# Attention, then two expert layers on one core: filler matmuls, decay products, state zeros and the order at attention's end are placed otherwise

## The chip, the cores and the metric

The kernel runs on one core of a Trainium2 chip. Five engines work side by side, each through its own list of instructions in the order in which they were written: PE (TensorE, matmuls and transposes), DVE (VectorE), ACT (ScalarE), POOL (GpSimd) and SP (SyncE, which here only issues DMAs). The metric is device microseconds of one execution, lower is better. Rows of the profile count microseconds from the first instruction.

## The reference

Three layers in a row. Only their core is shown.

```python
# attention: B=2, H=8 heads, S=768 positions, D=48
for t in range(S):
    state = alpha[:, :, t, :, None] * state + einsum('bhd,bhe->bhde', k[:, :, t], v[:, :, t])
    y[:, :, t] = einsum('bhd,bhde->bhe', q[:, :, t], state)
x = y in rows of 384                       # 1536 tokens
# first expert layer: 8 experts, top 1, 384 -> 1024 -> 384
e = argmax(x @ w_gate); gate = softmax(x @ w_gate)[e]
x = gate * (relu(x @ w1[e]) @ w2[e])       # up to `capacity` tokens per expert
# second expert layer: noisy top 2 of 8
logits = x @ w_gate + log1p(exp(x @ w_noise)) * noise
out = sum over the 2 best experts of softmax weight * (relu(x @ w1[e]) @ w2[e])
```

## The kernel before

**Attention in chunks.** The positions of a batch are cut into 6 chunks of 128, so there are 12 chunks, numbered i = 0 to 11 (batch 0 first). Within a chunk the recurrence is turned into matrix products: `decays` makes running products of alpha with scans on DVE (one forward and one backward over each half chunk) and multiplies them into k and q. For one piece of the sequence (one, two or three chunks; the first has one chunk, then one, two, two, three and three) it issues, on DVE: a first scan and the product with k's first half (`times(V, k6, kn, w6, 0)`), a second scan and the product with q's second half, two small instructions, two more scans, and then the products of k's second half and q's first half with the last two scans. In the very first piece the product with q's second half comes late, so that three products stand in a row. A copy of the piece's chunk-start decays (`V.tensor_copy(z2v[:, :, 0], as_[:, m:])`) comes before the first scan, in the pieces for which ACT has not made it (`filled`).

**What a chunk does on PE.** `scores(i)` transposes the products of k (4 transposes) and multiplies k and q products (8 matmuls, each in the trace as two halves, so 16 rows); ACT copies both out, and GpSimd sets the upper triangle to zero (`affine_select`). `state(i)` updates the carried state, which ACT or DVE writes into `att`, a tile whose state part is set to zero at the start. `mix(i)` makes the chunk's output, copied out by ACT as `yT` (the line `A.activation(yT..., y[:HR, :], AF.Copy)`). `r1_logits(j)` multiplies `yT` of chunk j with an identity and the gate's weights; ACT copies the tokens out, and a DVE reduction (`gates`) makes the gate logits. `route1` then finds each token's expert and its row in eight steps (maximum, index and one-hot on DVE; an exponential on ACT; ranks on PE; sums on DVE; and the scatter of the rows to DRAM by indirect DMAs from GpSimd).

**The order.** Nothing is scheduled by a program: `PATTERNS[i]` is a string per chunk, and each letter issues one thing: S scores of the next chunk, D a step of the decays, T the state, L the logits of chunk i - 1, R a step of the routing, W a quarter of a split of the first expert's weights (ACT copies the high part, GpSimd or DVE makes the low part by subtraction), M the mix. `FXR` is such a string for the end of attention: x a step of `first_x` (which gathers the first expert's tokens on PE: three steps for the early chunks' rows, then one per late chunk 8 to 11), R a routing step, l the logits of chunk 11. Because every engine works its list in order, a letter's place decides what stands behind it on all engines.

**The fillers.** `warm(n)` issues n matmuls of 512 columns on a tile of zeros; nothing reads them. `WARM0` of them stand at the start, `WARM2` = 10 behind the first scores, `FILL` behind chunk 0's mix, `WARM1` = 2 at the end of attention.

**The expert layers.** Behind attention each layer works expert by expert: the hidden product, then the second product, both with weights split into a high and a low part (three matmuls for one). The change leaves these layers alone.

Of the kernel before, what the change touches and what calls it, by code (L numbers as in the profile page):

```python
# [12 lines left out]
ALU = mybir.AluOpType  # L13
# [5 lines left out]
HR = 112  # L19
# [11 lines left out]
P1 = C1 // T1  # L31
R = N
SPARE = E * R
WARM0 = 34
NF, ND = F // 128, DM // 128
IW = HR + E
PIECES = [(0, 0, 2), (0, 2, 2), (0, 4, 2), (1, 0, 3), (1, 3, 3)]
# [2 lines left out]
MASKS = "G" * 12  # L40
STATES = "AAAAAAAAVVVV"
DECAYS = "444444440000"
FILL = (20,)
S0 = 1
WARM1 = 2
WARM2 = 10
FXR = "xRRxRRlxRRRRRxxRxRR"
EARLY = 8
WE = "GGGGVVVVVVVVVGGG"
PATTERNS = (  # L50
    "SDDTDDM", "SDDTLDDM", "SDDTLDDM", "SDDTLRRRDDM", "SDDTLDDM", "SRRDTLRRRDDDM",
    "SDDTLRRRDDM", "WSDDTWLDDMW", "WSRRWTRRRWLRRRWMW", "RWSRWTRRRWLWMW", "STLRRRWWMW", "RRRRRLRRRM")
LATE = (0, 4)
LZ = 0
LR = (5, 6, 7, 5, 7, 8)
# [12 lines left out]
def body(tc, ap, cap, dbg=False, stop=False):  # L68
    nc = tc.nc
    V, A, G, PE = nc.vector, nc.scalar, nc.gpsimd, nc.tensor  # L70
    with ExitStack() as ctx:
# [46 lines left out]
        qkv, vts = {}, {}  # L118

        piece_of, room = {}, {}  # L120
        a_at, at_ = {}, 0
# [4 lines left out]
        def load_piece(b, c0, n):  # L126
            parts_ = PARTS[PIECES.index((b, c0, n))]
            w = n * 512
            a6, k6, q6 = s6([128, w + sum(1 + 8 * m for _, _, m in parts_)]), s6([128, w]), s6([128, w])
            oa = o = 0  # L130
            for (b, c, m) in parts_:
                wa, v = 520 * m + 1, m * 512
                mine = (a6[:, oa:oa + wa], *(x[:, o:o + v].rearrange("r (h j) -> r h j", h=2) for x in (k6, q6)))
                nc.sync.dma_start(mine[0], ap["as"][:, a_at[b, c]:a_at[b, c] + wa])
                at = 128 * 512 * (b * NC + c)
                for x, name in zip(mine[1:], ("ks", "qs")):
                    nc.sync.dma_start(x.rearrange("r h j -> r (h j)"),
                                      ap[name][at:at + 128 * v].rearrange("(r w) -> r w", w=v))
                qkv[b, c] = [x[:HR] for x in mine]
                room[b, c] = ((b, c0), o, w)  # L140
                for i in range(c, c + m):
                    piece_of[b, i] = (b, c)
                oa, o = oa + wa, o + v
# [8 lines left out]
        NCK = B * NC  # L152
# [20 lines left out]
        att = s6([128, 4 * IW + 128 + 8 * HR])  # L173
# [15 lines left out]
        z5 = const([HR, 12, 64], "z5")  # L189
        A.activation(z5, zs["z3"], AF.Copy)  # L190
        z2s = (zs["z2"], z5)
        V.memset(att[:HR, 4 * IW + 128:], 0.0)
        warm(WARM0)
        load_v(*PIECES[0])
        for a in PIECES[1:3]:
# [28 lines left out]
        begun, filled = [], []  # L224

        def decays(b, c0, n):
# [12 lines left out]
            w1v = w6[:, 0].rearrange("r (s j) -> r s j", j=64)  # L239
            w2v = w6[:, 1].rearrange("r (s j) -> r s j", j=64)  # L240

            def times(eng, src, dst, x, h):
                o = dst.rearrange("r (s h j) -> r s h j", h=2, j=64)[:, :, h, :]
                eng.tensor_tensor(o, src[:, h].rearrange("r (s j) -> r s j", j=64),
                                  x[:, h].rearrange("r (s j) -> r s j", j=64), op=ALU.mult)

            first, k_ = not begun, len(begun)
            z2v = z2s[k_ % 2][:, :m, :]
            z2 = z2v.rearrange("r s j -> r (s j)")
            if (b, c0) not in filled:  # L250
                V.tensor_copy(z2v[:, :, 0], as_[:, m:])
            begun.append((b, c0))
            V.tensor_tensor_scan(w6[:, 0, ::-1], a6[:, 1:w + 1][:, ::-1], z1[:, ::-1], 0.0, op0=ALU.mult, op1=ALU.add)
            times(V, k6, kn, w6, 0)
            yield
            V.tensor_tensor_scan(w6[:, 1], a6[:, w:2 * w], z2, 0.0, op0=ALU.mult, op1=ALU.add)
            if not first:
# [12 lines left out]
                                 op0=ALU.mult, op1=ALU.add)  # L270
            if first:
                times(V, q6, qn, w6, 1)
            times(V, k6, kn, v6, 1)
            yield
            times(V, q6, qn, v6, 0)
            if todo and todo[0][:2] in qkv:
                b2, c2, n2 = todo[0]
                filled.append((b2, c2))
# [100 lines left out]
        def r1_logits(j, first=True):  # L379
            js, row, l, k = grp[j]  # L380
            yT = yTs.pop(j)
            lg = pm()
            lv = lg[:, :4 * IW].rearrange("p (g n) -> p g n", g=4)
            for gp in range(4):
                PE.matmul(lv[:, gp, :], yT[:, gp, :], idw[:, gp, :], start=True, stop=True)  # L385
            def gates():
                V.tensor_reduce(l[:, k, :], lv[:, :, HR:].rearrange("p g n -> p n g"), axis=AX.X, op=ALU.add)


            if j == NCK - 1:  # L390
                gates()
            by = lambda x: x.rearrange("p (g a e) -> p g a e", g=4, a=2)
            for ab in range(2):
                A.activation(by(row[:, k, :DM])[:, :, ab, :], lv[:, :, ab * 64:ab * 64 + 48], AF.Copy)
            if j < NCK - 1:
                gates()
            if j >= EARLY and first:
                t = late[j] = sb([128, 2 * DM + C1], "b6", 5, F32R)
                A.activation(t[:, :DM], row[:, k, :DM], AF.Copy)
                G.tensor_tensor(t[:, DM:2 * DM], row[:, k, :DM], t[:, :DM].bitcast(F32), op=ALU.subtract)  # L400
            if dbg:
                nc.sync.dma_start(ap["xdbg"][j * 128:(j + 1) * 128], row[:, k, :DM])
# [653 lines left out]

        si_, slots = hb([128, C1], I32), hb([128, C1])
        G.iota(si_, pattern=[[1, C1]], base=0, channel_multiplier=0)
        A.activation(slots, si_, AF.Copy)
        for i in range(S0):  # L1060
            need(i)
# [483 lines left out]
```

## Time and profile before

| | |
|---|---|
| time, median of 3 runs | 455.93 us (455.37 to 456.27) |
| profiled execution | 457.59 us, of which its span 456.0 us |
| PE busy | 445.1 us, 98% of the span |
| GpSimd busy | 347.6 us, 76% |
| DVE busy | 273.0 us, 60% |
| ACT busy | 266.3 us, 58% |
| mean granted TensorE clock | 0.994 |
| DMA | 93.66 MB, mean 205 GB/s |

The span runs from the first to the last instruction of the profiled execution; 1.59 us lie around it. Attention takes PE until about 90 us, the first expert layer until about 242 us, the second until the end. A busy share is a mean over stages: PE counts as busy while a matmul waits in its queue for data, so that a small wait inside attention shows in the start times of matmuls, not as idle time.

### The profile page before, as it was taken

Reading aid. Unit: us, or ns where it says so; the run is one execution under the profiler, and the core shown is the slowest. Engines: PE = TensorE matmul, PEld = TensorE weight load, DVE = VectorE, ACT = ScalarE, POOL = GpSimd, SP = SyncE. Lnnn points to the kernel's source line nnn. Section 1 sums busy time; section 2 is a strip of 40 time slices with the busy share of each in tenths; the row PEclk is TensorE's granted clock in tenths of the full one; section 3 lists DMA queues with packets and bytes.
Section 4 is the critical chain, followed back from the end, with each engine's and each line's share of the span. In section 5 each row is a group of like instructions: output and inputs, shape, how many; then the busy total and the mean of one; then the engine's idle time right before and its main releaser. Section 6 shows DMA issues by size and latency. Waiting matters only on the chain.

```text
span 456.0 us, 9516 instructions
## 1 busy us (share of the span) xinstructions
PE 445.1 (98%) x3167; PEld 418.4 (92%) x3170; DVE 273.0 (60%) x906; ACT 266.3 (58%) x703; POOL 347.6 (76%) x436
## 2 busy tenths in 40 slices
PE   8999999999999999999999999999999999999992
PEld 3688888899999999999999999999999999999992
DVE  8989986856967867878866454333443343243350
ACT  3577787467776776786651468255473464664310
POOL 3434697785998989999943379989989698799922
PEclk9999999999999999999999999999999999999997
DMA  8974972869999987876321997649287492993232
GB/s 284 407 269 150 327 260 96 259 199 313 329 307 314 269 253 224 269 226 193 123 70 55 253 324 229 136 108 323 57 262 154 129 293 57 284 246 51 27 45 43
DMA packets 73586, 93.66 MB, mean 205 GB/s; under 512 B 31962, under 2 KB 56610, under 8 KB 73526
## 3 DMA queue, kind: packets, MB, share of 16 engines
q1 hardware_dynamic: 66854, 79.98, 57.4%
q0 software_dynamic: 6672, 12.97, 12.7%
q8 instruction: 27, 0.44, 0.4%
q14 instruction: 33, 0.27, 0.2%
HBM read 70.30 MB, written 20.02 MB: 198 GB/s over the span
## 4 chain that ended last, share of the span: by engine, by line
PE 95%; DMA 1%; ACT 1%; POOL 0%; DVE 0%; issue 0%; POOLq 0%; ACTq 0%
PE ph L683 24%; PE py L722 22%; PE ph L686 12%; PE py L714 8%; PE py L716 4%; PE ph L170 4%; PE ph L309 3%; PE pm L750 3%; PE pm L385 2%; PE py L336 2%; PE py L362 2%; PE py L356 2%; DMA s<-w 1%; PE py L303 1%; PE ph L1002 1%; PE ph L975 1%
## 5 line engine op out<-in xcount | busy, mean ns | idle before, releaser
L538 POOL TENSOR_TENSOR s<-s,s 128x384 fp32r<-128x384 f32 x211 | 221.1, 1169 | 17.9 <-ACT s L537 16.3
L683 PE MATMUL ph<-x,s 128*128 128x240 f32 (+9 forms) x768 | 133.1, 308 | 0.3 <-DVE h L693 0.2
L537 ACT ACTIVATE s<-s 128x384 fp32r<-128x384 f32 x256 | 124.9, 517 | 9.5 <-DMA s<-w 7.6
L683 PEld LDWEIGHTS ph<-x,s 128*128 128x128 f32 x768 | 116.2, 189 | 1.9 <-DVE h L693 0.4
L693 DVE SCALAR_TENSOR_TENSOR h<-ph,h 128x240 fp32r<-128x240 f32 (+9 forms) x128 | 60.2, 470 | 82.8 <-ACT h L692 80.7
L692 ACT ACTIVATE h<-ph 128x240 fp32r<-128x240 f32 (+9 forms) x128 | 54.1, 423 | 75.7 <-PE ph L686 70.6
L686 PE MATMUL ph<-x,s 128*128 128x240 f32 (+9 forms) x384 | 76.2, 306 | 0.0
L158 POOL DMA_INDIRECT out<-b,m_ix x28 | 44.0, 1571 | 29.4 <-ACT b L878 9.7
L722 PE MATMUL py<-h,s 128*128 128x304 f32 (+4 forms) x360 | 65.4, 339 | 0.0
L722 PEld LDWEIGHTS py<-h,s 128*128 128x128 f32 x360 | 63.2, 188 | 0.8
L714 PE MATMUL py<-h,s 128*128 128x480 f32 (+3 forms) x192 | 61.5, 376 | 0.0
L686 PEld LDWEIGHTS ph<-x,s 128*128 128x128 f32 x384 | 60.9, 189 | 0.2
L716 PE MATMUL py<-h,s 128*128 128x240 f32 (+3 forms) x192 | 50.5, 263 | 0.0
L318 POOL TENSOR_SCALAR_AFFINE_SELECT h<-h 128x512 f32<-128x512 f32 x24 | 22.8, 975 | 30.2 <-ACT h L317 30.2
L158 POOL DMA_INDIRECT xs<-b,m_si x32 | 32.5, 1017 | 17.0 <-DVE pm L832 10.6
L722 PE MATMUL py<-s,h 128*128 128x384 f32 x216 | 38.6, 337 | 0.0
L714 PEld LDWEIGHTS py<-h,s 128*128 128x128 f32 x192 | 36.1, 188 | 2.6
L722 PEld LDWEIGHTS py<-s,h 128*128 128x128 f32 x216 | 37.8, 188 | 0.0
L716 PEld LDWEIGHTS py<-h,s 128*128 128x128 f32 x192 | 36.6, 191 | 0.0
L636 DVE TENSOR_TENSOR x<-pm,x 128x384 fp32r<-128x384 f32 (+8 forms) x42 | 19.9, 473 | 25.8 <-ACT x L635 24.8
L538 DVE TENSOR_TENSOR s<-s,s 128x384 fp32r<-128x384 f32 x45 | 30.6, 700 | 0.4 <-ACT s L537 0.2
L635 ACT ACTIVATE x<-pm 128x384 fp32r<-128x384 f32 (+8 forms) x42 | 17.7, 421 | 22.3 <-DVE pm L632 19.0
(263 smaller groups left out, 606.0 us busy)
## 6 DMA issues: line engine op xcount, KB each, us to landing
s<-w SPq DMA_DIRECT2D x28, 768.0 KB
s<-w_2b SPq DMA_DIRECT2D x22, 768.0 KB
s<-w_1b SPq DMA_DIRECT2D x14, 768.0 KB
xs<-s SPq DMA_DIRECT2D x2, 1576.0 KB
out<-s SPq DMA_DIRECT2D x4, 768.0 KB
b<-xs SPq DMA_DIRECT2D x12, 156.0 KB
b<-xs SPq DMA_DIRECT2D x12, 144.0 KB
b<-b SPq DMA_DIRECT2D x44, 36.0 KB
```

Of the source, the lines that this page charges most:

```text
L158: st = G.indirect_dma_start(out=dst, out_offset=bass.IndirectOffsetOnAxis(ap=ix, axis=0), in_=src, in_offset=None, **kw)
L318: G.affine_select(a_, a_, pattern=[[0, 4], [1, 128]], compare_op=ALU.is_ge, fill=0.0, base=0, channel_multiplier=-1)
L537: A.activation(hi[sl], t[sl], AF.Copy)
L538: rest.append(lambda: (eng or V).tensor_tensor(lo[sl], t[sl], hi[sl].bitcast(F32), op=ALU.subtract))
L636: rest.append(lambda: V.tensor_tensor(xl[:, d, :], y[:, :c], xh[:, d, :].bitcast(F32), op=ALU.subtract))
L683: PE.matmul(p, w, x[:, d, :], start=(k == 0), stop=False)
L686: PE.matmul(p, w1_of(n, f, d)[0], xl[:, d, :], start=False, stop=(d == ND - 1))
L692: A.activation(hh, p, AF.Relu)
L693: V.scalar_tensor_tensor(hl, p, 0.0, hh.bitcast(F32), op0=ALU.max, op1=ALU.subtract)
L714: PE.matmul(yp[o][:, :2 * c], wh[:, sl], both, start=(f == 0), stop=(f == NF - 1), skip_group_check=True)
L716: PE.matmul(yp[o][:, :c], wl[:, sl], hh, start=False, stop=(f == NF - 1), skip_group_check=True)
L722: PE.matmul(out_, l, r, start=(f == 0 and k == 0), stop=(f == NF - 1 and k == 2))
```

## The change

Seven edits, all in attention:

1. `WARM0` goes from 34 to 22 fillers and `FILL` from 20 to 23.
2. The state part of `att` is set to zero by GpSimd, behind its index patterns, no longer by DVE ahead of the first scan.
3. In the first piece the transfer of alpha is issued as two, 257 and 264 columns; the first scan reads the first of them only. All later issues of SP stand one place further back.
4. The copy of the chunk-start decays comes behind the first scan and the first product.
5. In the pieces (0, 2) and (1, 3) the last two products are made in four: k and q of the piece's first chunk, then k and q of the rest.
6. The gate reduction of chunk 9 comes ahead of ACT's copies, as it did for chunk 11.
7. In chunk 10 the mix comes ahead of two quarter splits; in chunk 11 the logits come one routing step earlier; at attention's end the second step of `first_x` comes two routing steps earlier.

```diff
--- before.py
+++ after.py
@@ -31,7 +31,9 @@
 P1 = C1 // T1
 R = N
 SPARE = E * R
-WARM0 = 34
+WARM0 = 22
+FIRST = (9, 11)
+AHEAD = ((0, 2), (1, 3))
 NF, ND = F // 128, DM // 128
 IW = HR + E
 PIECES = [(0, 0, 2), (0, 2, 2), (0, 4, 2), (1, 0, 3), (1, 3, 3)]
@@ -40,16 +42,16 @@
 MASKS = "G" * 12
 STATES = "AAAAAAAAVVVV"
 DECAYS = "444444440000"
-FILL = (20,)
+FILL = (23,)
 S0 = 1
 WARM1 = 2
 WARM2 = 10
-FXR = "xRRxRRlxRRRRRxxRxRR"
+FXR = "xxRRRRlxRRRRRxxRxRR"
 EARLY = 8
 WE = "GGGGVVVVVVVVVGGG"
 PATTERNS = (
     "SDDTDDM", "SDDTLDDM", "SDDTLDDM", "SDDTLRRRDDM", "SDDTLDDM", "SRRDTLRRRDDDM",
-    "SDDTLRRRDDM", "WSDDTWLDDMW", "WSRRWTRRRWLRRRWMW", "RWSRWTRRRWLWMW", "STLRRRWWMW", "RRRRRLRRRM")
+    "SDDTLRRRDDM", "WSDDTWLDDMW", "WSRRWTRRRWLRRRWMW", "RWSRWTRRRWLWMW", "STLRRRMWWW", "RRRRLRRRRM")
 LATE = (0, 4)
 LZ = 0
 LR = (5, 6, 7, 5, 7, 8)
@@ -131,7 +133,8 @@
             for (b, c, m) in parts_:
                 wa, v = 520 * m + 1, m * 512
                 mine = (a6[:, oa:oa + wa], *(x[:, o:o + v].rearrange("r (h j) -> r h j", h=2) for x in (k6, q6)))
-                nc.sync.dma_start(mine[0], ap["as"][:, a_at[b, c]:a_at[b, c] + wa])
+                for k in ((0, 256 * m + 1), (256 * m + 1, wa)) if not qkv else ((0, wa),):
+                    nc.sync.dma_start(mine[0][:, k[0]:k[1]], ap["as"][:, a_at[b, c] + k[0]:a_at[b, c] + k[1]])
                 at = 128 * 512 * (b * NC + c)
                 for x, name in zip(mine[1:], ("ks", "qs")):
                     nc.sync.dma_start(x.rearrange("r h j -> r (h j)"),
@@ -189,7 +192,6 @@
         z5 = const([HR, 12, 64], "z5")
         A.activation(z5, zs["z3"], AF.Copy)
         z2s = (zs["z2"], z5)
-        V.memset(att[:HR, 4 * IW + 128:], 0.0)
         warm(WARM0)
         load_v(*PIECES[0])
         for a in PIECES[1:3]:
@@ -239,19 +241,19 @@
             w1v = w6[:, 0].rearrange("r (s j) -> r s j", j=64)
             w2v = w6[:, 1].rearrange("r (s j) -> r s j", j=64)
 
-            def times(eng, src, dst, x, h):
-                o = dst.rearrange("r (s h j) -> r s h j", h=2, j=64)[:, :, h, :]
-                eng.tensor_tensor(o, src[:, h].rearrange("r (s j) -> r s j", j=64),
-                                  x[:, h].rearrange("r (s j) -> r s j", j=64), op=ALU.mult)
+            def times(eng, src, dst, x, h, at=slice(None)):
+                o = dst.rearrange("r (s h j) -> r s h j", h=2, j=64)[:, at, h, :]
+                eng.tensor_tensor(o, src[:, h].rearrange("r (s j) -> r s j", j=64)[:, at],
+                                  x[:, h].rearrange("r (s j) -> r s j", j=64)[:, at], op=ALU.mult)
 
             first, k_ = not begun, len(begun)
             z2v = z2s[k_ % 2][:, :m, :]
             z2 = z2v.rearrange("r s j -> r (s j)")
-            if (b, c0) not in filled:
-                V.tensor_copy(z2v[:, :, 0], as_[:, m:])
             begun.append((b, c0))
             V.tensor_tensor_scan(w6[:, 0, ::-1], a6[:, 1:w + 1][:, ::-1], z1[:, ::-1], 0.0, op0=ALU.mult, op1=ALU.add)
             times(V, k6, kn, w6, 0)
+            if (b, c0) not in filled:
+                V.tensor_copy(z2v[:, :, 0], as_[:, m:])
             yield
             V.tensor_tensor_scan(w6[:, 1], a6[:, w:2 * w], z2, 0.0, op0=ALU.mult, op1=ALU.add)
             if not first:
@@ -270,9 +272,16 @@
                                  op0=ALU.mult, op1=ALU.add)
             if first:
                 times(V, q6, qn, w6, 1)
-            times(V, k6, kn, v6, 1)
-            yield
-            times(V, q6, qn, v6, 0)
+            if (b, c0) in AHEAD:
+                times(V, k6, kn, v6, 1, slice(0, 4))
+                times(V, q6, qn, v6, 0, slice(0, 4))
+                yield
+                times(V, k6, kn, v6, 1, slice(4, None))
+                times(V, q6, qn, v6, 0, slice(4, None))
+            else:
+                times(V, k6, kn, v6, 1)
+                yield
+                times(V, q6, qn, v6, 0)
             if todo and todo[0][:2] in qkv:
                 b2, c2, n2 = todo[0]
                 filled.append((b2, c2))
@@ -387,12 +396,12 @@
                 V.tensor_reduce(l[:, k, :], lv[:, :, HR:].rearrange("p g n -> p n g"), axis=AX.X, op=ALU.add)
 
 
-            if j == NCK - 1:
+            if j in FIRST:
                 gates()
             by = lambda x: x.rearrange("p (g a e) -> p g a e", g=4, a=2)
             for ab in range(2):
                 A.activation(by(row[:, k, :DM])[:, :, ab, :], lv[:, :, ab * 64:ab * 64 + 48], AF.Copy)
-            if j < NCK - 1:
+            if j not in FIRST:
                 gates()
             if j >= EARLY and first:
                 t = late[j] = sb([128, 2 * DM + C1], "b6", 5, F32R)
@@ -1056,6 +1065,7 @@
 
         si_, slots = hb([128, C1], I32), hb([128, C1])
         G.iota(si_, pattern=[[1, C1]], base=0, channel_multiplier=0)
+        G.memset(att[:HR, 4 * IW + 128:], 0.0)
         A.activation(slots, si_, AF.Copy)
         for i in range(S0):
             need(i)
```

On DVE, at the very start of the program: the state tile is `s_4_80`, the tile of ones and zeros that feeds the first scan `s_6_89`, the alphas `s_1_71`; a scan is listed as SCALAR_TENSOR_TENSOR. Before:

```order
L186 MEMSET s_6_89 112x1536
L188 MEMSET s_6_89 112x12
L192 MEMSET s_4_80 112x896
L251 COPY s_6_89<-s_1_71 112x4
L253 SCALAR_TENSOR_TENSOR s_26_200<-s_1_71,s_6_89 112x256
L244 TENSOR_TENSOR s_28_202<-s_2_72,s_26_200 112x4x64
L256 SCALAR_TENSOR_TENSOR s_26_200<-s_1_71,s_6_89 112x256
```

And with the change, where the same tiles are called `s_6_90` and, for the scan's and product's results, `s_26_189` and `s_28_191`:

```order
L189 MEMSET s_6_90 112x1536
L191 MEMSET s_6_90 112x12
L253 SCALAR_TENSOR_TENSOR s_26_189<-s_1_71,s_6_90 112x256
L246 TENSOR_TENSOR s_28_191<-s_2_72,s_26_189 112x4x64
L256 COPY s_6_90<-s_1_71 112x4
L258 SCALAR_TENSOR_TENSOR s_26_189<-s_1_71,s_6_90 112x256
```

The setting to zero has left DVE's list, and the copy stands behind the first product.

On DVE, at the end of the decays of piece (0, 2), whose results the scores of chunk 2 read (`s_45` is k's product, `s_46` q's). Before:

```order
L269 SCALAR_TENSOR_TENSOR s_44_293<-s_10_134,s_7_91 112x512
L244 TENSOR_TENSOR s_45_294<-s_11_135,s_44_293 112x8x64
L244 TENSOR_TENSOR s_46_295<-s_12_136,s_44_293 112x8x64
L283 TENSOR_TENSOR t_152<-s_10_134,s_43_292 112x4x2
L284 COPY t_154<-s_43_292 112x4x2
```

And with the change:

```order
L271 SCALAR_TENSOR_TENSOR s_44_282<-s_10_122,s_7_92 112x512
L246 TENSOR_TENSOR s_45_283<-s_11_123,s_44_282 112x4x64
L246 TENSOR_TENSOR s_46_284<-s_12_124,s_44_282 112x4x64
L246 TENSOR_TENSOR s_45_283<-s_11_123,s_44_282 112x4x64
L246 TENSOR_TENSOR s_46_284<-s_12_124,s_44_282 112x4x64
L292 TENSOR_TENSOR t_140<-s_10_122,s_43_281 112x4x2
```

The two products of 512 columns have become four of 256, those of chunk 2 first.

On ACT, around the mix of chunk 10 (`h_1188<-py_1175` is its `yT`, `s_210` the high part of a split, `m_ex` the routing's exponential for chunks 8 and 9). Before:

```order
L394 ACTIVATE s_204_1077<-pm_1147 128x4x48 x2
L399 ACTIVATE b_220_1155<-s_204_1077 128x384
L537 ACTIVATE s_210_1109<-s_135_760 128x384 x2
L365 ACTIVATE h_1188<-py_1175 112x512
L537 ACTIVATE s_210_1109<-s_135_760 128x384
L422 ACTIVATE m_ex_1161<-m_lm_1160 128x16
L394 ACTIVATE s_233_1214<-pm_1217 128x4x48 x2
```

And with the change, where `yT` is `h_1180`:

```order
L403 ACTIVATE s_204_1073<-pm_1143 128x4x48 x2
L408 ACTIVATE b_220_1151<-s_204_1073 128x384
L374 ACTIVATE h_1180<-py_1167 112x512
L546 ACTIVATE s_210_1105<-s_135_755 128x384 x3
L431 ACTIVATE m_ex_1157<-m_lm_1156 128x16
L403 ACTIVATE s_233_1206<-pm_1209 128x4x48 x2
```

The copy of `yT` no longer stands behind two splits, and the exponential now stands behind three instead of one.

## Rows read from the trace of the kernel before

**Rows 1.** The profile's page, chain that ended last, shares of the span by engine:

```profile
PE 95%; DMA 1%; ACT 1%; POOL 0%; DVE 0%; issue 0%; POOLq 0%; ACTq 0%
```

**Rows 2.** Timeline of PE's weight loads, 4 to 12 us: start, us, what, idle before:

```profile
6.62 0.15 PEld L170 LDWEIGHTS <-warm 128*128 128x128 bf16 x1 [0.27 <-issue]
7.05 4.27 PEld L170 LDWEIGHTS <-warm 128*128 128x128 bf16 x20 [0.28 <-issue]
11.44 0.55 PEld L303 LDWEIGHTS py<-iw,s 112*128 112x128 f32 x4
```

**Rows 3.** Timeline of PE, start of scores' products (L309) and the second fillers:

```profile
15.87 1.16 PE L309 MATMUL ph<-s,s 48*128 48x128 f32 x16
...
18.94 4.49 PE L170 MATMUL ph<-warm 128*128 128x512 bf16 x19
...
23.74 1.16 PE L309 MATMUL ph<-s,s 48*128 48x128 f32 x16
...
47.14 1.16 PE L309 MATMUL ph<-s,s 48*128 48x128 f32 x16
```

**Rows 4.** Timeline of DVE, the products that scores wait for, and one wait:

```profile
12.41 0.76 DVE L244 TENSOR_TENSOR s<-s,s 112x256 f32<-112x256 f32 x2
...
21.18 1.30 DVE L244 TENSOR_TENSOR s<-s,s 112x512 f32<-112x512 f32 x2
...
28.71 0.19 DVE L387 TENSOR_REDUCE m_l<-pm 128x8 f32<-128x32 f32 x1 [1.91 <-ACT s L394]
...
44.06 2.51 DVE L244 TENSOR_TENSOR s<-s,s 112x768 f32<-112x768 f32 x2
```

**Rows 5.** Timeline of DVE in the first piece:

```profile
2.95 0.81 DVE L192 MEMSET s<- 112x896 f32 x1
3.75 0.19 DVE L251 COPY s<-s 112x4 f32<-112x4 f32 x1
3.83 0.68 DVE L253 TENSOR_TENSOR_SCAN s<-s,s 112x256 f32<-112x256 f32 x1
4.55 0.42 DVE L244 TENSOR_TENSOR s<-s,s 112x256 f32<-112x256 f32 x1
...
7.41 1.07 DVE L244 TENSOR_TENSOR s<-s,s 112x256 f32<-112x256 f32 x3
```

**Rows 6.** Timeline of SP's DMA issues, the first two:

```profile
0.95 0.41 SPq L134 DMA_DIRECT2D s<-as  x1
1.41 0.42 SPq L137 DMA_DIRECT2D s<-ks  x1
```

**Rows 7.** What the DMA queues moved in the first 4 us:

```profile
DMA packets 309, 0.58 MB, mean 144 GB/s; under 512 B 30, under 2 KB 30, under 8 KB 309
```

**Rows 8.** Timeline of POOL and DVE, one scan form with and without GpSimd beside it:

```profile
13.99 2.06 POOL L318 TENSOR_SCALAR_AFFINE_SELECT h<-h 128x512 f32<-128x512 f32 x2 [8.48 <-ACT h L317]
...
15.48 1.65 DVE L256 TENSOR_TENSOR_SCAN s<-s,s 112x512 f32<-112x512 f32 x1
...
24.61 1.22 DVE L256 TENSOR_TENSOR_SCAN s<-s,z 112x512 f32<-112x512 f32 x1
```

**Rows 9.** Timeline of ACT, DVE and PE at attention's end:

```profile
79.29 0.92 ACT L537 ACTIVATE s<-s 128x384 fp32r<-128x384 f32 x2
80.25 0.60 ACT L365 ACTIVATE h<-py 112x512 f32<-112x512 f32 x1
81.15 0.21 ACT L422 ACTIVATE m_ex<-m_lm 128x16 f32<-128x16 f32 x1
...
81.65 0.15 DVE L432 TENSOR_REDUCE m_se<-m_ex 128x2 f32<-128x16 f32 x1
...
80.89 1.15 PE L385 MATMUL pm<-s,h 112*128 112x120 f32 x8 [0.20 <-ACT h L365]
...
85.25 1.06 PE L385 MATMUL pm<-s,h 112*128 112x120 f32 x8
```

**Rows 10.** Busy time in the last stretch, with the granted clock (0.84) behind the engines:

```profile
440.00:456.00 16.00, 7.59 (x44) 7.11 (x42) 3.87 (x25) 0.42 (x1) 4.58 (x5) 0.84 0.31 44
```

## The prediction

> **What bounds the kernel now.** I read the chain of work that ended last first, to see which engine the end of the kernel hangs on: PE has 95% of it [rows 1]. PE's list therefore sets the time, and an edit is worth what it takes off that list or out of its waits. The list also holds fillers that nobody reads. The second view is the timeline of their weight loads. Before 7.05 us they come 0.43 us apart (6.62 to 7.05), the pace of 512 columns at 1.2 GHz; from 7.05 on, 20 of them take 4.27 us, 0.2135 each, which is 2.4 GHz [rows 2]. PE had been busy with fillers alone when its clock rose. So 14 of the 34 are slow and 20 fast, and the first scores start at 11.44, right behind the last filler.
>
> The third view is when PE comes to the products of the scores and when DVE has the data. The first scores read the three products that end at 8.48 (7.41 + 1.07) [rows 5], and PE comes 3 us later. Chunk 1's data end at 13.17 (12.41 + 0.76) and PE starts their products at 15.87; chunk 2's end at 22.48 and PE comes at 23.74; chunk 6's end at 46.57 and PE comes at 47.14 [rows 3, 4]. So the data are early by 2.7, 1.26 and 0.57 us. DVE cannot run ahead without end, though: at 28.71 it has waited 1.91 us for ACT, whose work follows PE's logits [rows 4].
>
> **The change part by part.** I work in microseconds of the profiled execution (457.59, a span of 456.0 and 1.59 around it); it is 1.66 above the median of 455.93, and I carry the difference over to the median.
>
> *Fewer fillers at the start.* The 12 that go are all of the fast part, since the 14 slow ones come first: 12 x 0.2135 = 2.56 off PE's list [rows 2]. PE would be through with the other 22 at 8.88. The first scores' data are there at 8.48 with DVE as it was, so nothing takes the fillers' place there.
>
> *Three more fillers behind chunk 0.* 3 x 0.2135 = 0.64 back. They stand with the 20 that PE runs through from 18.94 [rows 3].
>
> *DVE's first piece.* Setting the states to zero leaves DVE's list (0.81), the copy (0.08 from its start to the next) moves behind, and the first scan, at 3.83, could start right behind the small setting to ones, at about 2.9 [rows 5]. It needs half of alpha's transfer, the product at 4.55 needs all of k's. Upper bound of DVE's gain: 0.9, if no transfer holds it. Lower bound: a loss of 0.5, since the added DMA pushes k's issue, and every later one of SP, back by one place of 0.46 (0.95 to 1.41) [rows 6], and the trace does not show how early k landed before 4.55. I take a gain of 0.3: in the first 4 us the queues moved 0.58 MB [rows 7], and alpha and k of the first piece are 0.53 MB of it, so k's last bytes come at about 3.9 and its product starts at about 4.2 instead of 4.55. The copy then stands in DVE's way for its 0.08, which it did before too. SP's other issues come the same 0.46 later; chunk 1's products were 2.7 ahead of PE.
>
> The Trainium skill, "DMA: Bandwidth & Descriptors", in the part on fixed and variable cost, puts some 2.0 us on every DMA plus its bytes at 436 GB/s. By it the half transfer would land at 0.95 + 2.0 + 0.3 = 3.25 and the whole at 3.56, an estimate: the split would bring only 0.3, and k, pushed back a place, would land at about 4.5; DVE's gain would be nothing and the sum 0.1 to 0.2 smaller. No row here gives a landing time, so the trace does not decide between them.
>
> *Zeros on GpSimd.* GpSimd sits idle for 8.48 before its first masks at 13.99 [rows 8]; the masks come 2.56 earlier and still leave 5.9 for a setting to zero that took DVE 0.81 [rows 5]. ACT writes the states only after chunk 0's state, so nobody waits. Without that cover it would delay chunk 0's mix by 0.8. If it slows a DVE scan beside it, the nearest row is a scan beside masks, 1.65 against 1.22 [rows 8]: a loss of 0 to 0.43; I take 0, since DVE's gain is bounded by k's landing first.
>
> *Masks beside other DVE work.* This is a cost that the list does not show. GpSimd's two masks of chunk 0 (13.99 to 16.05) follow PE's scores, so they move to about 11.4 to 13.5, onto the scans and products that chunk 1's scores read. A scan beside them lost 0.43 [rows 8]. I charge DVE 0 to 0.9 there and take 0.5: chunk 1's data end at 13.17 - 0.3 + 0.5 = 13.4, while PE, 2.56 earlier, comes to them at 13.31. A stall of 0.1, and with the transposes half a microsecond ahead of it, which read the first of the two products, about 0.2. DVE does not lose the 0.5 again behind, where the masks stood before.
>
> *Four products instead of two.* Four of 256 columns at 0.36 each (three in 1.07 [rows 5]) take 1.43 against 1.21 for two: 0.2 more for DVE, but chunk 2's two are done after 0.72 instead of 1.21 and more. Their end was 22.48; now 21.18 + 0.72 = 21.9, less 0.3: 21.6 [rows 4]. PE comes at 23.74 - 2.56 + 0.64 + 0.2 = 22.0 [rows 3]. No stall; without the split it would be 0.2.
>
> *The middle of attention.* From here on everything is 1.72 earlier on PE (2.56 - 0.64 - 0.2). DVE's wait at 28.71 ends when ACT is done, so 1.72 earlier, at 27.0; DVE itself is there at 26.8 - 0.3 + 0.2 = 26.7 [rows 4]. Behind it DVE works without a pause up to chunk 6's products, whose 0.57 of slack stays. Chunk 9's part gets earlier by its own four products.
>
> *Attention's end.* PE's logits of chunk 10 wait for `yT`, which ACT copies from 80.25 on, right behind two splits of 0.92 together [rows 9]. With the mix ahead, ACT can start as soon as PE's mix is through, and that is hardly sooner, since PE has only the short rank products between the mix and the logits at 80.89: a gain of 0.05 to 0.1. In exchange the exponential stands behind three splits, from about 80.8 + 3 x 0.46: 82.1 instead of 81.15, and DVE's sum, which waits for it, comes at 82.35 instead of 81.65 [rows 9]. That pushes DVE's chain for chunk 10 by up to 0.7, and the ranks of chunk 10, which PE needs before the logits of chunk 11 at 85.25. The second step of `first_x`, now ahead of the ranks, gives PE work meanwhile. The gate reduction of chunk 9 ahead of ACT moves the one-hot forward by ACT's two copies, but it is not what the logits at 80.89 waited for: that was ACT's `yT` [rows 9]. Bounds for the whole: -0.5 to +0.4; I take a loss of 0.1.
>
> *The sum.* -2.56 + 0.64 + 0.2 + 0.1 = -1.6. The expert layers start that much earlier; their transfers and splits are all triggered by PE's and DVE's progress and not by a fixed time, so they keep their distances. 455.93 - 1.6 = 454.3.
>
> **The rivals.**
>
> *DVE keeps PE waiting.* PE gets to chunk 1 and 2 earlier and finds the data late: k lands a place later (0.5 lost), the masks cost 0.9 and the four products 0.2. Chunk 2's data then end at 21.9 + 0.5 + 0.9 = 23.3, and PE comes there 0.4 earlier than before, not 1.9. Gain 0.4: 455.5, no change that can be measured (below 0.2%, 0.9 us, none is). For it: DVE's scans and products stand close behind each other up to there, and the slack of chunk 1 is used up. Against: all bounds at once are needed. The same time comes out if the expert layers give the gain back, on GpSimd, busy 76%; against that is the chain, where POOL has 0% [rows 1]. Together 17%. By the rule of the Trainium skill's "DMA: Bandwidth & Descriptors" above, k would land late, which is one of the three things that this rival needs; no row here shows a landing.
>
> *Attention's end shortens too.* The one-hot is earlier, PE has the `first_x` steps to fill with, and GpSimd's scatter no longer stands ahead of chunk 10's low part. Upper bound 0.5 at the end, with no stall at chunk 1 (0.2) and the 0.1 not lost: -2.56 + 0.64 - 0.5 = -2.4: 453.5. Against: ACT's three splits. 13%.
>
> *The clock falls.* Fewer fillers leave PE less to do before 21 us. If it sat idle at 8.88 for want of data, the clock could drop to 1.2 GHz. From 11.44 to 23.74 PE works 12.3; the fillers among it (30, 6.4 us) take twice as long, the rest up to twice: 6 to 12 lost against 1.6 gained, some 461 to 466, slower. It decides if PE stands idle there. For it: the one stretch with a lower mean, 0.84, is that in which PE is busy 7.59 of 16 [rows 10]. Against: the data are there 0.4 ahead of PE, and behind 23.74 PE runs whole chunks without fillers at full pace, the same 1.16 for chunk 6's products as for chunk 2's [rows 3]. 6%.
>
> **How the numbers follow.** The forecast, a gain of 0.9 to 2.2, has 64%; the shorter end 13%; DVE or the layers behind it taking it back 17%; slower 6%, the clock among it. Faster by over 0.2% (below 455.0): 64 + 13 - 1 = 76%; within: 18%; slower: 6%. Two cases of the same sign hold most, so the range goes from the shorter end with 0.6 more (452.9) through the forecast's own range, 453.7 to 455.0, to the rival with almost no gain, 455.8.
>
> **What will show it.** The filler row at the start should end near 8.9 and the first scores' products start near 9.6; chunk 2's near 22.0; DVE's first scan near 3 and its first product near 4.2; DVE's wait at 28.71 should be gone or short. The logits of chunk 10 should start near 79.2 and those of chunk 11 near 83.6 to 83.7. Wrong I would be if the clock rises later than 7.05 in this execution, if k lands late, or if the layers behind attention wait for something that does not start earlier.

## The result, and the profile after

The change made the kernel slower: a median of 462.59 us over six runs (461.20 to 462.75) against 456.10 for the kernel before (455.37 to 457.32) in the same series. The medians are 6.5 us apart. The ratio of the runs is 1.013, 95% interval 1.0109 to 1.0151, which is some 5.9 us lost where the prediction had 1.6 gained; losses below go by such ratios. The profiled run took 461.28 us with a span of 459.6, the second shortest of the six. It shows a mild case: its mean granted clock is 0.990, while the four runs of 462.50 to 462.75 us have 0.983 to 0.987.

Read the traces in the prediction's order. The chain of work that ended last first, from the page: PE's 95% [rows 1] has become

```profile
PE 84%; DVE 8%; SPq 2%; DMA 2%; ACT 1%; issue 1%; POOL 0%; POOLq 0%; DVEq 0%; ACTq 0%
```

so that DVE now stands in the way somewhere. The timeline of DVE in the first piece (start, us, what, and in brackets the idle time before it and what ended it) answers to [rows 5]:

```profile
3.28 0.69 DVE L253 TENSOR_TENSOR_SCAN s<-s,s 112x256 f32<-112x256 f32 x1 [0.46 <-DMA s<-as]
5.71 0.43 DVE L246 TENSOR_TENSOR s<-s,s 112x256 f32<-112x256 f32 x1 [1.74 <-DMA s<-ks]
...
8.93 1.07 DVE L246 TENSOR_TENSOR s<-s,s 112x256 f32<-112x256 f32 x3
```

The scan is 0.55 earlier, the product behind it 1.16 later, because k has not landed; the three products are 1.52 later. PE, through with its fillers at 9.0, waits for them, and again at chunk 1. With the 0.64 of the added fillers that uses up the 12 fillers' 2.56 us by chunk 2, whose products started at 23.74 before [rows 3]. The timeline of PE:

```profile
9.81 0.57 PE L312 MATMUL py<-iw,s 112*128 112x112 f32 x4 [0.81 <-DVE s L246]
...
14.88 0.60 PE L312 MATMUL py<-iw,s 112*128 112x112 f32 x4 [1.13 <-DVE s L246]
...
23.93 1.16 PE L318 MATMUL ph<-s,s 48*128 48x128 f32 x16
```

The shift stays at +0.19 up to chunk 9's scores (62.50 against 62.31), so up to here the gain is missing and nothing more is lost. Then PE stops at the ranks of chunks 3 to 5. The timeline of PE there:

```profile
62.50 1.16 PE L318 MATMUL ph<-s,s 48*128 48x128 f32 x16
64.97 0.17 PE L435 MATMUL pm<-eb,ones 1*128 1x24 bf16 x1 [1.31 <-DVE m_l L396]
...
66.41 0.19 PE L438 MATMUL pm<-m_oh,ones 128*128 128x16 bf16 x2 [1.16 <-DVE m_oh L429]
...
72.93 1.16 PE L318 MATMUL ph<-s,s 48*128 48x128 f32 x16
```

The kernel before has no wait listed there. (The page hardly tells: PE's busy share goes from 98% to 97%.) DVE is late with the one-hot, and why shows in the timelines of DVE and GpSimd in this stretch, the kernel before first:

```profile
58.82 2.51 DVE L244 TENSOR_TENSOR s<-s,s 112x768 f32<-112x768 f32 x2
61.26 0.60 DVE L283 TENSOR_TENSOR t<-s,s 112x12 f32<-112x12 f32 x1
...
61.98 0.49 DVE L287 TENSOR_TENSOR gt<-t,t 112x12 f32<-112x12 f32 x1
...
63.38 0.21 DVE L420 TENSOR_TENSOR m_oh<-io,m_j 128x24 bf16<-128x24 f32 x1
...
57.93 4.52 POOL L318 TENSOR_SCALAR_AFFINE_SELECT h<-h 128x512 f32<-128x512 f32 x4
62.42 1.00 POOL L538 TENSOR_TENSOR s<-s,s 128x384 fp32r<-128x384 f32 x1
```

and the changed kernel:

```profile
59.31 3.51 DVE L246 TENSOR_TENSOR s<-s,s 112x256 f32<-112x256 f32 x4
62.75 0.98 DVE L292 TENSOR_TENSOR t<-s,s 112x12 f32<-112x12 f32 x1
...
63.89 0.92 DVE L296 TENSOR_TENSOR gt<-t,t 112x12 f32<-112x12 f32 x1
...
65.70 0.66 DVE L429 TENSOR_TENSOR m_oh<-io,m_j 128x24 bf16<-128x24 f32 x1
...
58.42 3.86 POOL L327 TENSOR_SCALAR_AFFINE_SELECT h<-h 128x512 f32<-128x512 f32 x4
62.26 1.43 POOL L547 TENSOR_TENSOR s<-s,s 128x384 fp32r<-128x384 f32 x1
...
63.80 1.94 POOL L547 TENSOR_TENSOR s<-s,s 128x384 fp32r<-128x384 f32 x2
```

(The row of four merges two products of 256 columns and two of 512.) The same columns as four products take 1.00 more than as two, beside GpSimd's four masks, which themselves take 0.66 less and end 0.17 sooner. The small products then fall beside GpSimd's splits: 0.98 for 0.60, 0.92 for 0.49, 0.66 for 0.21. The one-hot starts 2.32 later; 0.49 of that is DVE's later start on the products. Behind PE's idle time its clock falls. The stretches show the busy time of PE, its weight loads, DVE, ACT and GpSimd, and behind them the granted clock:

```profile
62.00:66.00 4.00, 1.95 (x24) 1.53 (x23) 3.96 (x16) 3.05 (x9) 4.00 (x6) 1.00 0.77 228
66.00:68.00 2.00, 1.59 (x16) 1.28 (x16) 0.46 (x2) 0.92 (x3) 1.91 (x4) 1.00 1.05 391
68.00:72.00 4.00, 4.00 (x29) 3.75 (x30) 3.66 (x22) 0.96 (x3) 1.78 (x3) 0.57 0.58 212
```

From 68 to 72 us PE is busy throughout at a mean of 0.57 of full speed. From 69 to 71 us it is 0.50, the lower level of 1.2 GHz. In the stretch of the stall PE had been busy 1.95 of 4. Chunk 10's products start at 72.93 instead of 68.56: +4.37. At attention's end some 0.75 more goes [rows 9]; PE's timeline:

```profile
85.21 1.15 PE L394 MATMUL pm<-s,h 112*128 112x120 f32 x8 [0.49 <-ACT h L374]
90.29 0.17 PE L439 MATMUL pm<-m_oh,tri 128*128 128x8 bf16 x1 [0.62 <-DVE m_oh L429]
90.32 1.13 PE L394 MATMUL pm<-s,h 112*128 112x120 f32 x8
...
95.40 1.02 PE L692 MATMUL ph<-x,s 128*128 128x240 f32 x6
```

The logits are 4.32 and 5.07 later, the first hidden products 5.14 (90.26 before). The span ends only 3.6 later. From its first hidden products to those of the second expert layer, the kernel before took 139.92 us in its profiled execution (90.26 to 230.18), the changed one 137.88 (95.40 to 233.28). The change does not touch that layer. The profiled execution of the kernel before is 1.5 slower than the median of 456.10, so the loss of the change is larger than the two spans say.

### The profile page after: what moved, and what is told of

The parts are those of the page before. It is cut to its first block, busy times and chain, and to the rows that moved or that the text cites. A ratio compares the mean times of both kernels' runs of the same rounds, so it can differ in the third digit from the quotient of the medians.

```text
span 459.6 us, 9504 instructions
## 1 busy us (share of the span) xinstructions
PE 443.8 (97%) x3158; PEld 418.4 (91%) x3161; DVE 272.3 (59%) x909; ACT 267.9 (58%) x703; POOL 349.5 (76%) x437
## 4 chain that ended last, share of the span: by engine, by line
PE 84%; DVE 8%; SPq 2%; DMA 2%; ACT 1%; issue 1%; POOL 0%; POOLq 0%; DVEq 0%; ACTq 0%
PE ph L692 23%; PE py L731 19%; PE ph L695 12%; PE py L723 9%; PE py L725 4%; PE pm L759 3%; DVE s L246 2%; SPq L917 2%; PE pm L394 2%; PE ph L318 1%; PE py L365 1%; PE py L345 1%; PE ph L173 1%; DMA s<-w 1%; PE py L371 1%
## 5 line engine op out<-in xcount | busy, mean ns | idle before, releaser
L327 POOL TENSOR_SCALAR_AFFINE_SELECT h<-h 128x512 f32<-128x512 f32 x24 | 23.8, 1016 | 27.5 <-ACT h L326 27.5
L547 DVE TENSOR_TENSOR s<-s,s 128x384 fp32r<-128x384 f32 x45 | 28.1, 644 | 1.4 <-ACT s L546 1.2
```

Of the source, the lines that this page charges most:

```text
L327: G.affine_select(a_, a_, pattern=[[0, 4], [1, 128]], compare_op=ALU.is_ge, fill=0.0, base=0, channel_multiplier=-1)
L547: rest.append(lambda: (eng or V).tensor_tensor(lo[sl], t[sl], hi[sl].bitcast(F32), op=ALU.subtract))
```

## Experiments

Each was compared with the kernel before on the same chip; "ratio" is to that, with its 95% interval. Start times are those of one profiled execution each.

**Alpha in one transfer again** (edit 3 undone):

```
-for k in ((0, 256 * m + 1), (256 * m + 1, wa)) if not qkv else ((0, wa),):
-    nc.sync.dma_start(mine[0][:, k[0]:k[1]], ap["as"][:, ...])
+nc.sync.dma_start(mine[0], ap["as"][:, a_at[b, c]:a_at[b, c] + wa])
```

> The changed kernel with one edit undone: alpha of the first piece comes in one transfer again, so that k is the second issue of SP and not the third. Theory T (two separate losses): k's late landing (its product at 5.71 instead of 4.55) cost PE the 1.9 us that the fillers should have given; the rest, a stall at chunk 9 and a lower clock behind it, comes from the four products of piece (1, 3). By T this kernel loses only the first part: about 460.5 us, and the wait for the ranks near 64 us with the clock at half for some us stays. Rival R (one root): the late k makes DVE late everywhere, and the stall at chunk 9 is only its echo. By R: 454 to 455, no stall near 64 us.

461.75 us, ratio 1.0126 (1.0109 to 1.0143). k was there when DVE came to it (4.49), and chunk 2's products were a microsecond earlier, at 22.91. The stall at the ranks stayed, with waits of 1.29 and 1.16, and the granted clock was 0.50 from 66 to 72 us. So the late k is not the root. What was won in front went into a longer stretch at the low clock: chunk 10's products start at 73.48, later than the changed kernel's 72.93.

**Two products instead of four** (edit 5 undone):

```
-AHEAD = ((0, 2), (1, 3))
+AHEAD = ()
```

> The changed kernel with one edit undone: the last two products of the pieces (0, 2) and (1, 3) are two again, not four; alpha's transfer stays split. Theory T: chunk 2's scores come some 0.5 us later, but the stall behind chunk 9 (2.8 us of idle PE and a clock at half for 3.7 us) is gone: about 458.5. Rival R (the late k is the root): the stall near 64 us stays, 462 or more.

457.29 us, ratio 1.0031 (1.0017 to 1.0046): 4.5 us of the 5.9 are gone with this one edit, which takes the four products out of both pieces. DVE's timeline in piece (1, 3) reads as before the change:

```profile
59.44 2.51 DVE L246 TENSOR_TENSOR s<-s,s 112x768 f32<-112x768 f32 x2
...
63.98 0.22 DVE L429 TENSOR_TENSOR m_oh<-io,m_j 128x24 bf16<-128x24 f32 x1
```

PE's wait at the ranks is too short to be listed, and the clock stays at 1.00.

**The old end of attention** (edits 6 and 7 undone):

```
-FIRST = (9, 11)
+FIRST = (11,)
-FXR = "xxRRRRlxRRRRRxxRxRR"
+FXR = "xRRxRRlxRRRRRxxRxRR"
-    ... "STLRRRMWWW", "RRRRLRRRRM")
+    ... "STLRRRWWMW", "RRRRRLRRRM")
```

> The changed kernel with attention's end in the old order (edits 6 and 7 undone). In the trace of the change the stretch from the logits of chunk 10 to those of chunk 11 is 0.75 us longer than before, PE waiting 0.6 for the one-hot of chunk 10, whose chain on DVE stood behind an exponential that ACT made after three splits. Theory T: 0.7 us less, about 461.9. Rival: the end is only shifted by the earlier stall, and the old order gives no difference (within 0.3).

462.45 us, ratio 1.0146 (1.0129 to 1.0163): no gain. My theory, which took the 0.75 between the logits for a loss of the whole, falls for this kernel.

**The old fillers** (edit 1 undone: `WARM0` 34, `FILL` 20):

> The changed kernel with 34 and 20 fillers again. Theory T: PE waits for DVE at the first two chunks anyway (0.8 and 1.1 us idle), so the fillers that were taken out gave nothing and putting them back costs nothing: 462 to 463, the stall near 64 us unchanged. Rival C: the fillers taken out are themselves the cause, by leaving PE idle at 9 and 14 us and bringing the clock down: then this kernel is near 456.

461.95 us, ratio 1.0138 (1.0121 to 1.0155). The change is no better with 12 fillers less than without that edit. The waits at the ranks stay (1.56 and 1.16), so rival C falls: the fillers are not the cause.

**The four products alone**: the kernel before with `AHEAD = ((1, 3),)` and the branch that makes four products, nothing else.

> The kernel before with one thing added: the last two products of piece (1, 3) as four, 256 columns of each first and 512 of each behind. Theory T: it suffices for the loss: the products take about 3.5 in place of 2.51 beside GpSimd's masks, the one-hot comes 1 us or more later, PE waits 2 or more at the ranks of chunks 3 to 5, the clock falls to 0.5 of full speed for some us, 459 to 461. Rival I (it needs the other edits, which shift DVE against GpSimd): products below 3.0, no fall of the clock, 456 to 457.

460.06 us, ratio 1.0081 (1.0064 to 1.0098). The timelines of DVE and PE:

```profile
58.01 3.51 DVE L245 TENSOR_TENSOR s<-s,s 112x256 f32<-112x256 f32 x4
...
63.66 0.17 PE L434 MATMUL pm<-eb,ones 1*128 1x24 bf16 x1 [0.99 <-DVE m_l L395]
...
65.11 0.19 PE L437 MATMUL pm<-m_oh,ones 128*128 128x16 bf16 x2 [1.16 <-DVE m_oh L428]
```

The same 3.51, the same stall, the clock at 0.50 from 67 to 70 us: this part alone loses 3.7 us. No other edit is needed, and rival I falls.

**The changed kernel with alpha whole and four products only for (0, 2)**; beside it the same **with the old end too** (the edits as above):

> The change without its third edit (alpha in one transfer) and with the four products only for piece (0, 2), not for (1, 3). Theory T (the four products of (1, 3) beside GpSimd's masks make the one-hot late, PE stands idle before the ranks of chunks 3 to 5, and its clock falls there): no wait of more than 0.3 us at those ranks, granted clock 1.00 from 60 to 75 us, and the gain of the start, 0.84 in the run with alpha whole, stays up to chunk 10's scores; attention's end then loses 0.75 as in the changed kernel; sum about 456.0 (455.6 to 456.4). Rival N (some other part of the change makes the stall): the wait at the ranks stays over 1 us, the clock falls, 460 or more.

> As the run before, with the sixth and seventh edit undone too (gates of chunk 9 behind ACT's copies, the old two patterns and the old order of the low part). Theory T: with the stall gone the old order of attention's end gives its 0.75 back: about 455.2 (454.8 to 455.6), 0.5 to 0.9 below the run before. Rival: the new order costs nothing in an undisturbed kernel, as it did in the disturbed one: both runs within 0.3 of each other.

456.15 us, ratio 0.9997 (0.9980 to 1.0013), and 456.13, ratio 0.9998 (0.9989 to 1.0008). The first is what the theory said: no wait listed at the ranks of chunks 3 to 5, clock 1.00 from 60 to 75 us. Of the start's gain, 0.80 at chunk 2, 0.52 is left at chunk 10's products (68.04 against 68.56). In the second the rival is right: the old end put the logits of chunk 11 at 84.45 instead of 85.43, but PE then waited 0.71 for the one-hot of chunk 11, which the new end does not. The new end waits at the rank of chunk 10 instead. PE's timelines, the new end first:

```profile
85.41 0.17 PE L438 MATMUL pm<-m_oh,tri 128*128 128x8 bf16 x1 [0.62 <-DVE m_oh L428]
```

```profile
88.24 0.17 PE L438 MATMUL pm<-m_oh,tri 128*128 128x8 bf16 x1 [0.71 <-DVE m_oh L428]
```

The first hidden products start at 90.52 and 90.51. Edits 6 and 7 move a wait from the rank of chunk 11 to the rank of chunk 10.

**The fillers alone** (the kernel before with `WARM0 = 22`, `FILL = (23,)`):

> The kernel before with the first edit alone: 22 fillers ahead and 23 behind chunk 0 in place of 34 and 20. Theory T (what the fillers free, DVE takes: chunk 2's data end at 22.48 before, and the masks of chunk 0, now earlier, cost DVE 0 to 0.5 ahead of them): chunk 2's scores start at 22.6 to 23.1 and not at 21.8, 455.1 to 455.6, a gain of 0.4 to 0.9. Rival F, the prediction's own sum for this edit (2.56 less, 0.64 more): chunk 2's scores at 21.8, 454.1. Rival Z: no gain at all, within 0.3 of the kernel before.

455.39 us, ratio 0.9981 (0.9972 to 0.9991): the only measured gain, 0.9 us. Its ten runs lie between 455.25 and 455.63, those of the kernel before between 455.60 and 458.94; the shortest differ by only 0.35. Chunk 2's products start at 22.54, 1.20 earlier, close to my theory's 22.6; the first hidden products only 0.45 earlier (89.81). Where the rest goes is shown by the timelines of DVE, GpSimd and PE at attention's end:

```profile
85.64 0.97 DVE L418 TENSOR_TENSOR m_lm<-m_l,m_g 128x8 f32<-128x8 f32 x1
86.53 1.15 DVE L420 TENSOR_TENSOR m_oh<-io,m_j 128x8 bf16<-128x8 f32 x1
...
85.56 1.02 POOL L400 TENSOR_TENSOR b<-s,b 128x384 fp32r<-128x384 f32 x1
...
87.73 0.17 PE L430 MATMUL pm<-m_oh,tri 128*128 128x8 bf16 x1 [0.71 <-DVE m_oh L420]
```

Two instructions of 8 columns take a microsecond each beside GpSimd's low parts of chunks 10 and 11.

**Fewer fillers and four products for (0, 2)** (the kernel before with `WARM0 = 22` and `AHEAD = ((0, 2),)`):

> The kernel before with 22 fillers ahead, still 20 behind chunk 0, and the four products for piece (0, 2) alone. Theory T (four products cost little where GpSimd has nothing to do, 1.43 against 1.30, and bring chunk 2's data 0.5 forward; DVE's data bound the start): chunk 2's scores at 21.9 to 22.3, a gain of 1.4 to 1.8 there, of which attention's end gives some 0.4 back: 454.6 to 455.2, 0.2 to 0.8 below the run with 22 and 23 fillers alone. Rival: the ranks of chunk 11, which then wait for their one-hot, take all of it: within 0.3 of that run (455.4).

456.69 us, ratio 0.9989 (0.9976 to 1.0002). Chunk 2's products came at 22.17, as the theory said, but the rank of chunk 11 at 87.73 with a wait of 0.74, at the same time as in the run above. The gain in front ends there, as the rival said. The ratio is 0.0008, some 0.4 us, above that of the run above, with overlapping intervals; the rival had at most 0.3.

**No masks beside the products**, in the changed kernel; it leaves the scores of chunks 7 and 8 unmasked and puts five quarter splits off:

```
+if i in (7, 8):
+    continue
 G.affine_select(...)
-"WSRRWTRRRWLRRRWMW"
+"SRRTRRRLRRRM"
```

> The changed kernel with the masks of chunks 7 and 8 left out (their scores stay unmasked) and the splits of chunk 8's stretch put off to later ones, so that GpSimd has nothing to do while DVE makes the four products of piece (1, 3) and the small products behind them. Theory L (it is GpSimd beside it that makes each of these instructions longer): the four products take 1.9 to 2.2 in place of 3.51, the two small products behind them 0.2 to 0.3 each in place of 0.98 and 0.92, PE waits less than 0.5 at the ranks of chunks 3 to 5 and its clock stays at 1.00 there; 456 to 459, since the splits come later. Rival C (four instructions in place of two are slow by themselves): 3.3 or more, the stall and the fall of the clock stay.

Timelines of DVE, GpSimd and PE:

```profile
59.20 1.96 DVE L246 TENSOR_TENSOR s<-s,s 112x256 f32<-112x256 f32 x4
61.08 0.98 DVE L292 TENSOR_TENSOR t<-s,s 112x12 f32<-112x12 f32 x1
...
62.23 0.93 DVE L296 TENSOR_TENSOR gt<-t,t 112x12 f32<-112x12 f32 x1
...
60.86 1.17 POOL L549 TENSOR_TENSOR s<-s,s 128x384 fp32r<-128x384 f32 x1 [2.56 <-DMA xs<-s,m_si]
...
62.13 0.99 POOL L549 TENSOR_TENSOR s<-s,s 128x384 fp32r<-128x384 f32 x1
...
64.15 0.19 PE L440 MATMUL pm<-m_oh,ones 128*128 128x16 bf16 x2 [0.37 <-DVE m_oh L431]
```

The four products take 1.96 in place of 3.51; PE waits 0.37, its clock stays at 1.00, and chunk 10's products start at 69.06 in place of 72.93. Theory L is right on the products, and rival C falls: four in place of two are not slow by themselves. On the two small ones I was wrong, since two splits of an earlier stretch moved up beside them, and each is about as long as its split. The time of the whole, 462.94 us, misses the 456 to 459 expected: with the splits put off, the first expert layer takes 143.98 us, 2.74 of it a wait of PE at 97 us.

**Fillers in the stall.** The changed kernel with

```
 scores(si)
+if si == 9:
+    warm(10)
```

> The changed kernel with 10 fillers more, behind the scores of chunk 9 and so in the place where PE waits for the ranks' one-hot; 10 x 0.2135 = 2.1 of the 2.5 that it waits. Theory K (PE's idle time lets its clock fall, and that costs 1.6 beyond the wait itself): the one-hot comes as late as before, the granted clock stays 1.00 from 66 to 72 us, chunk 10's scores come 1.2 to 1.8 earlier, near 71.0: 460.8 to 461.4. Rival W (the wait alone costs): the clock makes no difference, 462.3 to 462.9.

461.14 us, ratio 1.0089 (1.0074 to 1.0105), against the change's 1.013 (1.0109 to 1.0151): 1.9 us back by more work on PE. (The profiled execution, 461.46, shows it only up to the first hidden products, at 93.74 instead of 95.40.) PE's timeline and the stretch from 68 to 72 us:

```profile
63.52 2.33 PE L173 MATMUL ph<-warm 128*128 128x512 bf16 x10
...
66.36 0.19 PE L438 MATMUL pm<-m_oh,ones 128*128 128x16 bf16 x2 [0.27 <-DVE m_oh L429]
...
71.27 1.16 PE L318 MATMUL ph<-s,s 48*128 48x128 f32 x16
```

```profile
68.00:72.00 4.00, 4.00 (x49) 3.56 (x49) 3.71 (x22) 1.66 (x5) 1.83 (x3) 1.00 0.58 213
```

The one-hot comes as late as in the changed kernel, the clock stays at 1.00, and chunk 10's products start 1.66 earlier. Theory K is right: of the 4.37, some 1.7 is the clock. A mean of 0.57 over the 4 us from 68 to 72 us is some 3.4 us at 0.50, and half of that is 1.7.

**The low part ahead of the scatters** (the run with the fillers alone, and in the last pattern `"RRRRRLRRRM"` to `"RRRRLRRRRM"`):

> The kernel before with 22 and 23 fillers, as the run with the fillers alone, and one letter of edit 7: the logits of chunk 10 one step earlier in the last pattern, which on GpSimd's list puts chunk 10's low part ahead of the scatters of chunks 8 and 9 and changes no other engine's order. In the run with the fillers alone that low part ran from 85.56 to 86.58, beside DVE's last subtraction and one-hot (0.97 and 1.15, uncontended 0.16 and 0.20), and PE waited 0.71 for them at the rank of chunk 11. Theory L (an instruction of GpSimd beside it makes each of DVE's with two inputs wait): the low part now runs near 82 to 83, the subtraction and one-hot take 0.2 each, the wait of 0.71 is gone, the first hidden products start near 89.1 in place of 89.81, 454.6 to 455.0, ratio 0.9965 to 0.998. Rival: the low part earlier meets DVE's products and sums of chunks 8 and 9 instead, which makes the one-hot late all the same: within 0.3 of the run with the fillers alone (ratio 0.998).

457.47 us, ratio 1.001 (0.9999 to 1.0021). Timelines of DVE, GpSimd and PE:

```profile
82.26 1.08 DVE L447 TENSOR_TENSOR acc<-acc,m_oh 128x8 bf16<-128x8 bf16 x2
...
86.52 0.17 DVE L420 TENSOR_TENSOR m_oh<-io,m_j 128x8 bf16<-128x8 f32 x1
...
82.06 1.06 POOL L400 TENSOR_TENSOR b<-s,b 128x384 fp32r<-128x384 f32 x1 [0.60 <-DVE b L442]
...
84.18 0.17 PE L430 MATMUL pm<-m_oh,tri 128*128 128x8 bf16 x1 [0.62 <-DVE m_oh L420]
```

The last one-hot now takes 0.17 instead of 1.15, but the two sums in front take 1.08 instead of 0.35, and PE waits 0.62 one rank earlier. The rival is right: the collision moved. The first hidden products start at 89.73, 0.08 earlier than with the fillers alone, so the further 1.3 us of the whole between these two arise behind attention. In the two traces the first expert layer takes 139.59 us (89.73 to 229.32) against 137.88 (89.81 to 227.69); what makes it longer was not followed.

## Why the prediction was wrong

**The step that failed** is "Four products instead of two": "0.2 more for DVE", applied to piece (0, 2) and waved through for the other piece with "Chunk 9's part gets earlier by its own four products". The price is right where GpSimd is idle beside them (the prediction has 1.21 for two, [rows 4] has 1.30). DVE's rows of piece (0, 2), with four products in the changed kernel and with two in the run with two products:

```profile
22.63 1.43 DVE L246 TENSOR_TENSOR s<-s,s 112x256 f32<-112x256 f32 x4
```

```profile
22.62 1.29 DVE L246 TENSOR_TENSOR s<-s,s 112x512 f32<-112x512 f32 x2
```

For piece (1, 3) it was 1.00, then some 1.3 more on small products that slid beside the splits, 2.5 of waiting on PE and 1.7 of clock. The prediction had the row to see it: chunk 6's two products of 768 took 2.51 at 44.06 [rows 4], where six times the 0.36 of 256 columns [rows 5] would give 2.2. Two masks of GpSimd ran beside them, from 43.15 to 45.76. It charged "masks beside other DVE work" at the start and nowhere else.

**The fillers**: the removal itself was sized rightly (PE was through at 9.0, foreseen 8.88). The sum was not: chunk 2's products came 1.20 earlier with the fillers alone (1.57 with 20 behind chunk 0 and the four products of (0, 2)), not 1.72, and attention's end kept only 0.45. In the run with the fillers alone PE waited for DVE 0.52 at chunk 0 and 1.13 at chunk 1, where the sum had nothing and 0.2. The charge for the masks was right: chunk 1's products started 0.45 later (12.86 against 12.41, 0.5 taken). In the change, nothing was left. That PE was through near 8.88 is partly luck: the slack came from one execution. The fillers' pace doubles at 7.05 us in it and at 6.62 in the changed kernel's (the page's clock row reads 1.00 throughout), but anywhere from 4.06 to 7.47 over all traces. The run with the four products alone has the front of the kernel before; its fillers speed up at 5.67, and its chunk 2 starts at 22.94. Against that run the fillers alone win 0.40 there, not 1.20.

**DVE's first piece**: the gain of 0.3 fell, and so did its lower bound, a loss of 0.5: the three products came 1.52 later in the profile. In six traces with the split, the product that needs k started at 4.88 to 5.74, waiting for k each time; in eight with alpha whole, the kernel before among them, at 4.45 to 4.55 with no wait. The Trainium skill's "DMA: Bandwidth & Descriptors" (fixed and variable cost) fits its cost to DMAs that GpSimd issues; these are SP's. The prediction's estimate from it (3.25 for half of alpha, 3.56 for the whole, 4.5 for k) is near these traces for alpha, where the scan that waits for it starts at 3.16 to 3.28 and at 3.73 to 3.79; k came later. The cost to the whole was hidden under the stall; without the stall, alpha whole together with the four products for (0, 2) is worth 1.5 us (ratio 0.9997 against 1.0031).

**Zeros on GpSimd and the copy behind** were costed at nothing. They were not tried alone. With alpha whole and the zeros on GpSimd (three traces) the first scan waits for alpha till 3.73 to 3.79, so what the zeros gave back stood idle.

**Attention's end**: the loss of 0.1 for the whole was near enough; without the stall the new and the old end measure alike (ratios 0.9997 and 0.9998). The exponential went late as foreseen, but the wait only changes place.

**The rivals**: the time fell into the range of "the clock falls", 461 to 466, which had 6%. That is in part luck. The rival named the condition, PE idle for want of data, but put it at 8.88 us. PE did stand idle there, 0.81 and then 1.13, and chunk 0's and chunk 1's products still took 1.16: no fall. Where the clock fell, near 68 us, it cost 1.7 and not the 6 to 12 of the rival; the wait cost 2.5. "DVE keeps PE waiting" (17%) had k's late landing and PE's waits at chunks 0 and 1 right, and gave them no loss. The place where DVE had least slack behind a changed instruction was near 64 us. There DVE had less than 0.1 between the one-hot (63.38 + 0.21) and the rank that reads it (63.65), a row that I did not read.

**Open**: a part of the 5.9 (5.14 stand at the first hidden products in the profiled runs), and why kernels that start the expert layers within 0.3 us of each other (89.73 to 90.00) end up to 0.3% apart. The traces place it in the first expert layer, which lasts from 137.85 to 139.92 us in every run but the one without masks, the longest in the kernel before; no run here changed that layer, so its cause is not shown.

## What to carry to other kernels

Price a split of one instruction into several by the rows beside the engine that it shares a resource with, not by its columns: each piece can be held up again, and whatever is pushed back may slide beside the next long instruction. Look up, for each edit on a producer, the consumer with the least slack behind it, and count a stall of PE twice, as time and as clock (here 2.5 and 1.7 us). Read a slack from more than one execution. A gain at the start is only worth what the tightest wait further on lets through.

## What the hardware showed unexpectedly

An instruction of DVE with two inputs in SBUF, of 8 or 12 columns, took about as long as the GpSimd instruction beside it: 0.98 and 0.93 beside splits of 1.17 and 0.99, and 1.15 beside a low part's subtraction, for 0.16 to 0.2 without. DVE's reductions and searches (maximum, index) kept their 0.15 to 0.29 beside the same splits; an addition of a constant took 0.77 beside two splits in the kernel before, but 0.17 beside masks and 0.15 beside a low part. The Trainium skill, "SBUF — State Buffer", in the section on its two separate sides, states just this: a DVE instruction with two SBUF inputs and a GpSimd one that reads SBUF exclude each other for a whole instruction. These traces agree: beside the masks two products took 2.51 and four 3.51, and four took 1.96 without them.

PE's granted clock did not fall in the stall itself: the rows have 1.00 from 62 to 68 us, and 0.50 from 69 to 71, over work that ran without a pause. With ten fillers in the stall it stayed at 1.00.
